# A gated mix of a long-convolution layer and an MLP mixer: plain weight loads, early sines, evictions on ScalarE, and another order of the work

## The chip, the cores and the metric

The kernel runs on one core of a Trainium2 chip. The engines of a core work side by side, each through its own queue in order: TensorE (PE, with its weight load PEld), VectorE (DVE), ScalarE (ACT), GpSimd (POOL) and SyncE (SP), which issues most DMAs. ACT and POOL issue some as well. Waits between engines are semaphores that the framework sets from the data and from the reuse of buffers. The metric is the device time of one launch in microseconds, as the median of several runs.

## The reference

With x of 2048 positions by 640 columns (the batch is 1), all in bf16:

```python
g = sigmoid((x * gate_w).sum(-1))
# a: short causal convolution of k with 4 taps, times v, then a long convolution
kv = sum_t(k shifted by 3 - t, times shift_k) * v
y  = irfft(rfft(kv, 4096) * rfft(ssm_k, 4096))[:2048] + kv * ssm_D
a  = x * y
# b: mixer
h  = gelu(layernorm(x) @ w1)            # 640 -> 640
hs = concat(h[0:160] one later, h[160:320] one earlier,
            h[320:480] two later, h[480:640] two earlier) @ w2
x1 = x + hs
b  = x1 + gelu(layernorm(x1) @ w3) @ w4 # 640 -> 1536 -> 640
out = g * a + (1 - g) * b
```

## The kernel before

Position s = 16 p + n lies on partition p, in slot n. So x is 16 tiles u of 128 partitions by 640 columns, held in four tiles Q. The mixer goes over four chunks c of four slots. `norm_stats` (L275) makes mean and variance on DVE (the tiles st, mv) and the power on POOL (ve, rs). `norm_apply` (L288) makes xn on DVE, transposes it on PE into PSUM, and evicts it to XNT, in two pieces (4 and 1 of the 5 blocks of columns), on DVE or ACT by an argument. `first_product` (L331) multiplies by W1 in the column order "blocks 0 to 3 are the first 128 columns of the four shift groups, block 4 the last 32 of each". Its gelu writes blocks 0 to 3 with the shift straight into GS. Block 4 goes through a tile u4, whose four quarters POOL copies to GS. `second_product` (L413) multiplies GS by W2 and DVE adds the sum to Q. `third_product` (L425) makes gelu(. @ W3) into tiles G, and `fourth_product` (L440) multiplies by W4 and DVE adds to Q (L456), or makes the output at the end (L452). Groups of the last three are US[0] to US[3]: slots 2 to 5, 6 to 9, 10 to 13, and 14, 15, 0, 1.

The long convolution is a Fourier transform in two steps of matmuls. `filter_transpose` (L260) turns the five loaded tiles HN of the filter into HTA and HTB, and DROW (ssm_D) is added to its first tap. `short_conv` (L397) makes kv for one group of four slots on DVE, from KT, the taps CJ (POOL copies of a raw load CJR, which takes an XNT buffer) and KHALO (k of the slots before). `step1` (L237) multiplies by F1 for filter and signal: PE L246, eviction to AR on ACT (L90), and an ACT-queue DMA that writes DRAM, SH for the filter and SX for the signal. Sines for the second step are made by `gen_step2` (L190): DVE makes integers in three tiles GEN, and ACT makes M2, G1 and G2 by four sines each (L187). `spectrum` (L519) then loops over t = 0 to 31. `spec_h` (L469, matmul L478) makes the filter's spectrum HS from BH, which an SP DMA reads from SH, and swaps the halves of its partitions by another DMA (L483). `spec_x` (L485, matmul L491) makes the signal's from BX, evicts it to XPB on ACT and multiplies by HS on DVE (L496). `spec_z` (L499, matmul L507) goes back, and its tile psz is evicted to ZG by ACT and DVE in turn, and goes to DRAM (SZ). `y_group` (L552) reads SZ as ZT, makes the last matmuls (L564), and combines with g and Q. The gate takes x again as XQ, in the buffer of GS: `gate_dot` (L357) is one DVE instruction for each of 16 slots (row scr), `gate_act` makes g and 1 - g (OMG), and ACT scales Q by OMG.

Order: code is emitted in the order in which the program text asks for it, and a scheduler of the framework reorders a little between engines. `merge(a, b, ratio)` (L589) takes a step of generator a, then as many steps of b as a's cost times the ratio pays for. Pools give buffers in turn under a tag: the tag "w" has three large ones (W1 and W2 together, HTA, W3, W4, XPB), "b5" eleven of four slots, "g" three (HN, GEN, later G), "xnt" two. PSUM has two buffers under "pm" (the mixer) and two under "pc" (everything of the convolution). A tile waits until the last use of the one whose buffer it takes.

Before, `signal()` (L613) runs convolution g and, between its pieces, step 1 of g - 1. The filter's step 1 is merged with the second product of US[0], then come first products 2 and 3 with the first convolution and the sines, then a merge of `mixer_front` with the signal at 0.6, then the spectrum merged with a third and a fourth product at 0.75, and the rest of these is emitted after it. A third product follows the last psz, and then the y groups and the last fourth product.

Of the kernel before, what the change touches and what calls it, by code (L numbers as in the profile page):

```python
# [17 lines left out]
def kernel(  # L18
# [25 lines left out]
    nc = tc.nc  # L44
# [73 lines left out]
    load_q(0)  # L118
    load_h(0)
    load_q(1)  # L120
    load_h(1)
    W12 = weights("W12", [P, 2, DT, D])
    W1P = W12[:, 0]
    W2P = W12[:, 1]
    w1v = B_w1.rearrange("(kt p) n -> p kt n", p=P)
    pieces = [(gi * P, P, gi * CG) for gi in range(4)] + [(4 * P + gi * R, R, gi * CG + P) for gi in range(4)]
    with nc.allow_non_contiguous_dma(reason="weight permutation"):
        for (nn, cnt, oo) in pieces:
            nc.sync.dma_start(out=W1P[:, :, nn:nn + cnt], in_=w1v[:, :, oo:oo + cnt])
    load_h(2)  # L130
    load_q(2)
# [26 lines left out]
    def gen_tile():  # L158
        t = main.tile([P, 1024], I32, name="GEN", tag="g", bufs=3)
        return t[:]  # L160
# [29 lines left out]
    def gen_step2():  # L190
        GA, GB, GC = gen_tile(), gen_tile(), gen_tile()
# [13 lines left out]
        for name, kl in (("f", klf), ("i", kli)):  # L205
            ms = consts.tile([P, 2, 4], F32, name="ms" + name)
            for a, amp in ((0, 2 * PI_ / TU), (1, -PI_)):
                for j in range(4):
# [6 lines left out]
        nc.gpsimd.iota(ick.rearrange("p (g i n) -> p g i n", i=4, n=16), pattern=[[64, 8], [4, 4], [0, 16]],  # L215
                       base=0, channel_multiplier=0)
        nc.gpsimd.iota(icn.rearrange("p (m n) -> p m n", n=16), pattern=[[0, KH], [1, 16]],
                       base=0, channel_multiplier=0)
# [4 lines left out]
        yield 0.0  # L223
        nc.vector.scalar_tensor_tensor(out=m1, in0=ick, scalar=basei[:], in1=icn, op0=ALU.add, op1=ALU.mult)
# [31 lines left out]
    DROW = row("DROW")  # L256
    nc.gpsimd.dma_start(out=DROW[0:1, :], in_=A_ssm_D.rearrange("(a d) -> a d", a=1))
# [50 lines left out]
    for gi, sh in enumerate(shifts):  # L308
        for b in (range(0, sh) if sh > 0 else range(N2 + sh, N2)):
            col = 0 if sh > 0 else P - 1  # L310
            nc.gpsimd.memset(GS[:, gi, b, col:col + 1], 0.0)
            nc.gpsimd.memset(GS[gi * R:(gi + 1) * R, 4, b, col:col + 1], 0.0)
# [18 lines left out]
    def first_product(c, XNT):  # L331
        for nts in ((4,), (0, 1), (2, 3)):
            ps = ps_tile("psw1", "pm")
            for j, nt in enumerate(nts):
                for dt in range(DT):
                    nc.tensor.matmul(ps[:, j, :], lhsT=W1P[:, dt, nt * P:(nt + 1) * P], rhs=XNT[:, dt, :],  # L336
                                     start=(dt == 0), stop=(dt == DT - 1))
# [19 lines left out]
    def gate_dot(u):  # L357
        scr = row("scr")
        nc.vector.scalar_tensor_tensor(out=scr[:], in0=XQ[:, u, :], scalar=1.0, in1=GWB[:],  # L359
                                       op0=ALU.mult, op1=ALU.mult, accum_out=Z32[:, u:u + 1])  # L360
# [79 lines left out]
    def fourth_product(us, G, last):  # L440
        for i, u in enumerate(us):
# [13 lines left out]
            else:  # L455
                nc.vector.tensor_tensor(out=halves(qu), in0=ps[:, :, 0:HD], in1=halves(qu), op=ALU.add)  # L456
            yield 1.6
# [27 lines left out]
    def spec_x(t):  # L485
# [7 lines left out]
        xp = XPB[:, t % 4]  # L493
# [21 lines left out]

    AH = 5
    LAST = []

    def spectrum():  # L519
# [6 lines left out]
        for t in range(n):  # L526
# [4 lines left out]
            if t in (1, 2, 5, 6):  # L531
                g = (1, 2, 5, 6).index(t)
                nc.sync.dma_start(out=XQ[:, 4 * g:4 * g + 4, :], in_=qv[:, 4 * g:4 * g + 4, :])
            if 4 <= t < 4 + N2:
                gate_dot(t - 4)
            if t == 4 + N2:
                gate_act()
            if t > 4 + N2:
                done_ = [u for us in US[0:3] for u in us]
                for u in (done_[t - 5 - N2:t - 4 - N2] if t < n - 1 else done_[t - 5 - N2:]):  # L540
                    qu = Q[u // 4][:, u % 4, :]
                    evac("a", qu, qu, OMG[:, u:u + 1])
# [9 lines left out]
    def y_group(g, early):  # L552
# [6 lines left out]
        for i in range(4):  # L559
# [8 lines left out]
            nc.vector.tensor_tensor(out=ty[:], in0=ty[:], in1=XQ[:, u, :], op=ALU.mult)  # L568
            qu = Q[u // 4][:, u % 4, :]
            if u in early:  # L570
                evac("a", qu, qu, OMG[:, u:u + 1])
                nc.vector.tensor_tensor(out=qu, in0=qu, in1=ty[:], op=ALU.add)
            else:
                fin = edge("fin")
                nc.vector.tensor_tensor(out=fin[:], in0=qu, in1=ty[:], op=ALU.add)
                nc.sync.dma_start(out=outv[:, u, :], in_=fin[:])
# [12 lines left out]
    def merge(a, b, ratio):  # L589
# [11 lines left out]
        for _ in b:  # L601
            pass

# [9 lines left out]
    def signal():  # L613

        prev = iter(())
        for g in range(NG):
            if 1 < g + 1 < NG:
                load_kv(g + 1)
            if g == 1:
                nc.sync.dma_start(out=W4[:], in_=B_w4.rearrange("(kt p) e -> p kt e", p=P))  # L620
            for c_ in short_conv(g):
                yield c_
                next(prev, None)
                next(prev, None)
            run(prev)
            prev = step1(xrows(g), SX, g)
        for c_ in prev:
            yield c_

# [3 lines left out]

    c4 = [[4 * c + i for i in range(4)] for c in range(NG)]
    st0 = norm_stats(tiles_of(c4[0]))
    filter_transpose(0)
    X0 = norm_apply(tiles_of(c4[0]), st0, "v")
    st1 = norm_stats(tiles_of(c4[1]))
    CJ = load_cj()
    filter_transpose(1)  # L640
    with nc.allow_non_contiguous_dma(reason="weight permutation"):
        for (nn, cnt, oo) in pieces:
            nc.sync.dma_start(out=W2P[nn % P:nn % P + cnt, nn // P, :], in_=B_w2[oo:oo + cnt, :])
    load_h(3)
    load_q(3)
    KHALO = load_halo()
    load_h(4)
    load_kv(0)
    X1 = norm_apply(tiles_of(c4[1]), st1, "v")
    run(first_product(0, X0))  # L650
    filter_transpose(2)
    st2 = norm_stats(tiles_of(c4[2]))
    filter_transpose(3)
    run(first_product(1, X1))
    filter_transpose(4)
    W3 = weights("W3", [P, DT, Fh])
    nc.sync.dma_start(out=W3[:], in_=B_w3.rearrange("(kt p) f -> p kt f", p=P))
    load_kv(1)
    sig = signal()
    X2 = norm_apply(tiles_of(c4[2]), st2, "v")  # L660
    gen = gen_step2()
    next(gen)
    merge(second_product(US[0]), filt(), 1.0)
    next(sig)
    sy0 = norm_stats(tiles_of(US[0]))
    next(sig)
    run(first_product(2, X2))
    next(gen)
    st3 = norm_stats(tiles_of(c4[3]))
    next(sig)  # L670
    next(gen)
    Y0 = norm_apply(tiles_of(US[0]), sy0, "v")
    X3 = norm_apply(tiles_of(c4[3]), st3, "v")
    W4 = weights("W4", [P, FT, D])
    run(first_product(3, X3))

    def mixer_front():
# [4 lines left out]
        Y1 = norm_apply(tiles_of(US[1]), sy1, "v")  # L682
        yield 3.0
        yield from fourth_product(US[0], G_[0], False)
        yield from second_product(US[2])
        sy2 = norm_stats(tiles_of(US[2]))
        yield 4.4
        yield from third_product(Y1, G_[1])
        Ys.append(norm_apply(tiles_of(US[2]), sy2, "v"))
        yield 3.0  # L690
        yield from second_product(US[3])
        sy3 = norm_stats(tiles_of(US[3]))
        yield 4.4
        yield from fourth_product(US[1], G_[1], False)
        Ys.append(norm_apply(tiles_of(US[3]), sy3, "v"))

    Ys = []
    merge(mixer_front(), sig, 0.6)
    XPB = weights("XPB", [P, 4, 3, D])
    XQ = main.tile([P, N2, D], BF16, name="XQ", tag="gs")  # L700
    third3 = third_product(Ys[1], G_[3])
    merge(spectrum(), chain(third_product(Ys[0], G_[2]), fourth_product(US[2], G_[2], False)), 0.75)
    with tc.issue_after(LAST[-1].ins):
        run(third3)
# [33 lines left out]
```

## Time and profile before

| quantity | us |
|---|---|
| median of 3 runs | 320.95 |
| lowest, highest | 318.3, 322.01 |
| the profiled execution | 321.86 |
| its span | 320.1 |

The profile is of the execution of 321.86 us; 1.76 us of it lie outside the span. All times below are counted from the start of the span. The costliest groups of instructions on ACT, DVE and PE are:

| group (line, engine, tile) | count | busy us | mean ns |
|---|---|---|---|
| L445 PE, fourth product, 128x320 | 384 | 59.1 | 299 |
| L432 PE, third product, 128x512 | 240 | 56.9 | 391 |
| L90 ACT, AR from step 1, 128x640 | 64 | 40.3 | 694 |
| L496 DVE, XPB products, 128x640 | 64 | 28.5 | 487 |
| L326 ACT, gelu to G, 128x1024 | 24 | 24.8 | 1031 |
| L336 PE, first product, 128x512 | 100 | 27.9 | 434 |

A matmul's mean counts from its own issue and overlaps its neighbours, so that work is priced below by the spacing of instructions that follow each other without a wait. In a row of the timeline or of a group, "out<-in" names the tiles, "x8" counts the instructions, and the bracket at the end has the idle time before and what ended it.

Of transfers, the page gives the time from issue to landing: W (1920 KB) 12.7 us, SH<-AR 3.3, BX<-SX 5.1, BH<-SH 4.8, HS<-HS 2.6.

### The profile page before, as it was taken

To read this page: it belongs to the slowest core of one execution; us is meant where nothing else is said; L and a number is where in the kernel's file an instruction comes from. 1 tells how busy PE (TensorE), PEld (TensorE's weight loads), DVE (VectorE), ACT (ScalarE), POOL (GpSimd) and SP (SyncE) were. 2 spreads that over 40 slices of the span, in tenths; PEclk is the share of its full clock that TensorE was granted. 3 is DMA by queue.
4 is the path that set the end of the run, shared out by engine and by line. 5 is a ranking of instruction groups with operands and counts; after the bars stand their busy time and mean duration, and the time that the engine had idled before them with its cause. 6 is when DMAs were issued, how large, how long until landed. Compare 5 with 4: busy or idle time off the path is not lost.

```text
span 320.1 us, 4302 instructions
## 1 busy us (share of the span) xinstructions
PE 256.1 (80%) x1572; PEld 151.4 (47%) x1572; DVE 207.4 (65%) x433; ACT 174.3 (54%) x250; POOL 33.5 (10%) x68
## 2 busy tenths in 40 slices
PE   1538989762079999999989969999966664899995
PEld 1424565331045546764556634566633332445673
DVE  4889669711993983799988980465565554500982
ACT  1221559999715262226635048979876674445750
POOL 3362611500003110002001000000000000000000
PEclk9965999997559999999999989999997999599999
DMA  7999900679600242022227935487789865259741
GB/s 244 255 318 376 402 7 0 245 244 368 210 2 0 82 163 84 2 82 82 84 82 239 402 83 182 123 258 236 217 283 264 288 204 180 82 171 405 248 174 72
DMA packets 32787, 59.59 MB, mean 186 GB/s; under 512 B 7391, under 2 KB 23903, under 8 KB 32766
## 3 DMA queue, kind: packets, MB, share of 16 engines
q1 hardware_dynamic: 19870, 42.77, 40.9%
q10 hardware_dynamic: 12672, 15.73, 13.3%
q0 software_dynamic: 224, 0.82, 0.8%
q8 instruction: 12, 0.20, 0.3%
q14 instruction: 9, 0.07, 0.1%
HBM read 35.71 MB, written 18.35 MB: 169 GB/s over the span
## 4 chain that ended last, share of the span: by engine, by line
PE 51%; DVE 22%; DMA 9%; ACT 7%; issue 2%; DVEq 0%; SPq 0%; ACTq 0%
PE psw L432 13%; PE psw L445 10%; PE psw L336 8%; PE psz L507 6%; DVE acc L407 4%; PE psw L418 4%; DMA BX<-SX 4%; DMA SH<-AR 3%; DVE tmp L405 3%; PE psy L564 3%; ACT AR L90 3%; DMA XQ<-in_A_q_dram 3%; PE psx L491 2%; PE psh L478 2%; DVE scr L359 2%; ACT HS L92 2%
## 5 line engine op out<-in xcount | busy, mean ns | idle before, releaser
L445 PE MATMUL psw<-W,G 128*128 128x320 bf16 x384 | 59.1, 299 | 0.1
L432 PE MATMUL psw<-XNT,W 128*128 128x512 bf16 x240 | 56.9, 391 | 0.0
L90 ACT CAST AR<-ps 128x640 bf16<-128x640 f32 x64 | 40.3, 694 | 26.4 <-PE ps L246 26.1
L496 DVE TENSOR_TENSOR XPB<-XPB,HS 128x640 bf16<-128x640 bf16 x64 | 28.5, 487 | 33.5 <-ACT XPB L90 33.5
L445 PEld LDWEIGHTS <-G 128*128 128x128 bf16 x384 | 37.5, 98 | 15.7 <-issue 1.0
L326 ACT ACTIVATE G<-psw 128x1024 bf16<-128x1024 f32 x24 | 24.8, 1031 | 24.7 <-PE psw L432 24.7
L432 PEld LDWEIGHTS <-W 128*128 128x128 bf16 x240 | 24.1, 101 | 27.9 <-issue 3.2
L92 ACT ACTIVATE HS<-psh 128x640 bf16<-128x640 f32 x32 | 22.8, 719 | 23.3 <-PE psh L478 23.3
L301 PE MATMUL pst<-IDB,xn 128*128 128x128 bf16 x160 | 14.3, 253 | 22.1 <-DVE XNT L95 13.0
L280 DVE BATCH_NORM_STATS2 st<-Q 128x6 f32<-128x320 bf16 x64 | 27.5, 466 | 4.2 <-DMA Q<-in_A_q_dram 4.2
L336 PE MATMUL psw<-XNT,W 128*128 128x512 bf16 x100 | 27.9, 434 | 2.3 <-DVE XNT L95 2.3
L507 PE MATMUL psz<-XPB,G 128*128 128x320 bf16 x128 | 25.6, 328 | 4.9 <-ACT HS L92 3.1
L90 ACT CAST XPB<-psx 128x640 bf16<-128x640 f32 x32 | 22.4, 700 | 7.0 <-PE psx L491 6.8
L418 PE MATMUL psw<-W,GS 128*128 128x320 bf16 x160 | 22.7, 299 | 1.6 <-DVE XNT L95 1.0
L301 PEld LDWEIGHTS <-xn 128*128 128x128 bf16 x160 | 12.3, 114 | 24.5 <-issue 17.7
L491 PE MATMUL psx<-BX,M 128*128 128x320 bf16 x64 | 15.3, 324 | 7.8 <-DMA BX<-SX 3.1
L507 PEld LDWEIGHTS <-G 128*128 128x128 bf16 x128 | 13.4, 105 | 15.9 <-issue 9.6
L246 PEld LDWEIGHTS <-F 128*128 128x128 bf16 x128 | 12.2, 97 | 17.6 <-issue 10.7
L294 DVE TENSOR_SCALAR xn<-Q,mv,rs 128x640 bf16<-128x640 bf16 x32 | 15.8, 536 | 5.9 <-POOL rs L285 5.9
L418 PEld LDWEIGHTS <-GS 128*128 128x128 bf16 x160 | 15.6, 98 | 8.4 <-issue 2.2
L95 DVE CAST ZG<-psz 128x640 bf16<-128x640 f32 x16 | 13.1, 821 | 9.3 <-PE psz L507 9.3
L336 PEld LDWEIGHTS <-W 128*128 128x128 bf16 x100 | 10.9, 110 | 16.5 <-issue 9.0
(104 smaller groups left out, 335.6 us busy)
## 6 DMA issues: line engine op xcount, KB each, us to landing
SH<-AR ACTq DMA_DIRECT2D x8, 640.0 KB, 3.3
SX<-AR ACTq DMA_DIRECT2D x8, 640.0 KB, 3.1
BH<-SH SPq DMA_DIRECT2D x8, 640.0 KB, 4.8
HS<-HS SPq DMA_DIRECT2D x32, 160.0 KB, 2.6
BX<-SX SPq DMA_DIRECT2D x8, 640.0 KB, 5.1
SZ<-ZG ACTq DMA_DIRECT2D x8, 640.0 KB, 3.5
ZT<-SZ SPq DMA_DIRECT2D x8, 640.0 KB, 5.9
W<-in_B_w_dram SPq DMA_DIRECT2D x2, 1920.0 KB, 12.7
```

Source lines behind the costliest of these rows:

```text
L90: nc.scalar.copy(out=o, in_=i)
L92: nc.scalar.activation(out=o, in_=i, func=ACT.Copy, scale=scale)
L280: nc.vector.bn_stats(out=st[:, h, :], in_=src[i][:, h * HD:(h + 1) * HD])
L301: nc.tensor.transpose(out=pst[:, dd, i * P:(i + 1) * P], in_=xns[i][:, (d0 + dd) * P:(d0 + dd + 1) * P], identity=IDB[:])
L326: nc.scalar.activation(out=o, in_=i, func=ACT.Gelu_apprx_tanh)
L336: nc.tensor.matmul(ps[:, j, :], lhsT=W1P[:, dt, nt * P:(nt + 1) * P], rhs=XNT[:, dt, :], start=(dt == 0), stop=(dt == DT - 1))
L418: nc.tensor.matmul(ps[:, h, 0:HD], lhsT=GS[:, nt, u, :], rhs=W2P[:, nt, h * HD:(h + 1) * HD], start=(nt == 0), stop=(nt == DT - 1))
L432: nc.tensor.matmul(ps[:, j, :], lhsT=W3[:, dt, (f + j) * P:(f + j + 1) * P], rhs=XNT[:, dt, :], start=(dt == 0), stop=(dt == DT - 1))
L445: nc.tensor.matmul(ps[:, h, 0:HD], lhsT=G[ft // 4][:, ft % 4, i * P:(i + 1) * P], rhs=W4[:, ft, h * HD:(h + 1) * HD], start=(ft == 0), sto ...
L491: nc.tensor.matmul(ps[:, h, 0:HD], lhsT=M2[:, t].rearrange("p a b c -> p (a b c)"), rhs=BX[kg][:, i, h * HD:(h + 1) * HD], start=True, sto ...
L496: nc.vector.tensor_tensor(out=xp[:, 1 + a, :], in0=xp[:, 0, :], in1=HS[t // 2][:, a, t % 2, :], op=ALU.mult)
L507: mm = nc.tensor.matmul(pz[:, h, 0:HD], lhsT=gm[:, t].rearrange("p a b c -> p (a b c)"), rhs=XP[t][:, 1 + a, h * HD:(h + 1) * HD], start=( ...
```

## The change

- W1 comes in its own column order by one DMA, right behind the first part of x, instead of eight DMAs that permute it. The matmul reads the first 128 columns of each group as the slice `nt * CG` to `nt * CG + P`, and the last 32 of each group are gathered by one ACT copy into W1E. W2 comes by two DMAs instead of eight.
- `gen_step2` has its integers in a "w" buffer (GENW) instead of three "g" buffers, and is started before anything else: M2's sines come ahead of X0's eviction, G1's after it, G2's after X1.
- Every eviction of XNT goes to ACT instead of DVE.
- The memsets of GS's edges on POOL, DROW's load and the loads of CJ and KHALO come later, and the order of loads and first products is another.
- The four first products with the first second product come before the filter's step 1, which is now run together with the first two short convolutions in `conv_front`; x's step 1 follows it.
- W4's load goes from the SP queue to the ACT queue, behind the filter's last write.
- `mixer` holds all second products, third products 0 to 2 and fourth products 0 to 2, in another order. What is left of it when `conv_front` ends goes beside the spectrum (ratio 1.5). XQ is loaded by four POOL DMAs after the last second product.
- The gate dots are asked for from t = 14 instead of t = 4, and Q is scaled by OMG as soon as its tile is summed (`summed`, `scaled`).

```diff
+    W1N = W12[:, 0]
+    nc.sync.dma_start(out=W1N, in_=B_w1.rearrange("(kt p) n -> p kt n", p=P))
...
-        for (nn, cnt, oo) in pieces:
-            nc.sync.dma_start(out=W1P[:, :, nn:nn + cnt], in_=w1v[:, :, oo:oo + cnt])
...
+    nc.scalar.copy(out=W1E.rearrange("p k (g r) -> p k g r", r=R),
+                   in_=W1N.rearrange("p k (g c) -> p k g c", c=CG)[:, :, :, P:CG])
+    def w1_cols(dt, nt):
+        return W1E[:, dt, :] if nt == 4 else W1N[:, dt, nt * CG:nt * CG + P]
+    def load_w2():
+        nc.sync.dma_start(out=W2P[:, 0:4, :], in_=bass.AP(
+            tensor=B_w2.tensor, offset=B_w2[0, 0].offset, ap=[[D, P], [CG * D, 4], [1, D]]))
+        nc.sync.dma_start(out=W2P[:, 4, :], in_=bass.AP(
+            tensor=B_w2.tensor, offset=B_w2[P, 0].offset, ap=[[CG * D, 4], [D, R], [1, D]]))
...
+    GENW = main.tile([P, 3, 1024], I32, name="GEN", tag="w", bufs=3)
...
-        GA, GB, GC = gen_tile(), gen_tile(), gen_tile()
+        GA, GB, GC = GENW[:, 0, :], GENW[:, 1, :], GENW[:, 2, :]
...
+    def conv_front():
+        rows = filt()
+        for g in range(NG):
+            if 1 < g + 1 < NG:
+                load_kv(g + 1)
+            if g == 2:
+                nc.scalar.dma_start(out=W4[:], in_=B_w4.rearrange("(kt p) e -> p kt e", p=P))
+                rows = chain(step1(xrows(0), SX, 0), step1(xrows(1), SX, 1))
+            if g == 3:
+                rows = step1(xrows(2), SX, 2)
             for c_ in short_conv(g):
                 yield c_
-                next(prev, None)
-                next(prev, None)
-            run(prev)
+                for _ in range(4 if g < 3 else 2):
+                    next(rows, None)
+            if g > 0:
+                run(rows)
+        for c_ in step1(xrows(3), SX, 3):
             yield c_
...
+    gen = gen_step2()
+    next(gen)
     st0 = norm_stats(tiles_of(c4[0]))
...
-    X0 = norm_apply(tiles_of(c4[0]), st0, "v")
+    X0 = norm_apply(tiles_of(c4[0]), st0, "a")
+    gs_edges()
+    next(gen)
+    load_w2()
...
+    run(first_product(0, X0))
+    X1 = norm_apply(tiles_of(c4[1]), st1, "a")
+    next(gen)
+    CJ = load_cj()
...
+    run(second_product(US[0]))
+    run(first_product(2, X2))
...
+    def mixer():
         yield from second_product(US[1])
...
         yield from fourth_product(US[0], G_[0], False)
+        yield from third_product(Y1, G_[1])
         yield from second_product(US[2])
...
         yield from second_product(US[3])
+        Y2 = norm_apply(tiles_of(US[2]), sy2, "a")
...
+        XQ.append(main.tile([P, N2, D], BF16, name="XQ", tag="gs"))
+        for g in range(NG):
+            nc.gpsimd.dma_start(out=XQ[0][:, 4 * g:4 * g + 4, :], in_=qv[:, 4 * g:4 * g + 4, :])
         yield from fourth_product(US[1], G_[1], False)
+        yield from third_product(Y2, G_[2])
+        Ys[0] = norm_apply(tiles_of(US[3]), sy3, "a")
+        yield from fourth_product(US[2], G_[2], False)
+    merge(conv_front(), mix, 1.0)
+    XPB.append(weights("XPB", [P, 4, 3, D]))
+    merge(spectrum(), mix, 1.5)
+    run(mix)
     with tc.issue_after(LAST[-1].ins):
-        run(third3)
+        run(third_product(Ys[0], G_[3]))
```

## The prediction

> **What bounds it now.** I read the page's busy shares first, then the chain that ended last, and cut the span at the chain's own milestones: the end of the first second product (51.03 us), the first third product (106.2; its first matmul in the chain is at 106.35), the wait for XQ (169.95), the loop's first psz (201.84), the end of the psz that still have filler beside them (231.9) and the start of the last third product (279.84).
>
> ```profile
> PE 256.1 (80%) x1572; PEld 151.4 (47%) x1572; DVE 207.4 (65%) x433; ACT 174.3 (54%) x250; POOL 33.5 (10%) x68
> ...
> PEclk9965999997559999999999989999997999599999
> ...
> PE 51%; DVE 22%; DMA 9%; ACT 7%; issue 2%; DVEq 0%; SPq 0%; ACTq 0%
> ```
> PE is busiest, but only half of the chain is PE. Where the other half lies is seen stage by stage (columns: stretch, its length, busy time of each engine, granted clock, DMA share, GB/s):
>
> ```profile
> 0.00:51.03 51.03, 33.40 (x235) 22.27 (x236) 38.70 (x125) 17.34 (x26) 19.64 (x48) 0.87 0.74 251
> 51.03:92.71 41.68, 21.09 (x126) 11.43 (x126) 26.02 (x49) 34.45 (x48) 5.21 (x8) 0.80 0.59 205
> 92.71:106.20 13.49, 13.49 (x70) 7.24 (x70) 8.56 (x14) 5.36 (x10) 2.89 (x6) 0.84 0.13 32
> 106.20:169.95 63.75, 61.22 (x396) 36.61 (x394) 53.88 (x81) 27.88 (x37) 4.50 (x4) 1.00 0.22 77
> 169.95:201.84 31.89, 29.33 (x183) 17.11 (x181) 20.21 (x51) 15.30 (x24) 1.26 (x2) 0.95 0.64 226
> 201.84:231.90 30.06, 30.06 (x200) 19.31 (x200) 16.77 (x32) 26.21 (x41) 0.00 (x0) 1.00 0.74 222
> 231.90:279.84 47.94, 31.33 (x155) 15.90 (x153) 25.88 (x51) 29.19 (x46) 0.00 (x0) 0.87 0.68 217
> 279.84:320.10 40.26, 36.22 (x221) 21.58 (x219) 17.35 (x37) 18.57 (x23) 0.00 (x0) 0.97 0.58 213
> ```
> Three stretches leave PE unused: the first two (38 us idle) and the 48 us after the filler ran out (17 idle). Inside and just behind the second, the timeline's rows of PE (two) and ACT (two) show the hole (start, length, engine, line; in brackets the idle time before and its releaser):
>
> ```profile
> 89.13 2.29 PE L301 MATMUL pst<-IDB,xn 128*128 128x128 bf16 x20 [12.96 <-DVE XNT L95]
> 92.71 3.57 PE L336 MATMUL psw<-XNT,W 128*128 128x512 bf16 x8 [1.29 <-DVE XNT L95]
> ...
> 75.75 1.28 ACT L187 ACT_TABLE_LOAD   x1
> 77.04 9.16 ACT L187 ACTIVATE G<-GEN,msi 128x1024 bf16<-128x1024 int32 x8
> ```
> PE waits 13 us for an XNT eviction that stands behind a short convolution on DVE, with the sines on ACT meanwhile. The chain has, before that, "ACT AR" pieces and 9.96 us of SH's write (the convolution's buffers), and later "BX<-SX" 5.80 and 6.35 in the loop without filler.
>
> **Prices** (spacing of back-to-back instructions): matmul 0.136 us (320 wide), 0.216 (512), 0.427 at half clock; so a first product is 5.4 per four tiles, second 5.6, third 13.0, fourth 13.1, step 1 8.7 for the filter and 8.7 for x, one t of the spectrum 1.09. ACT: AR 0.63, gelu 0.95, sine 1.15, table load 1.28, an XNT eviction estimated from 128x512 (585 ns) and 128x1024 (1031) at 1.9 + 0.6. DVE: convolution 10 per group, Q add 0.73.
>
> **To the end of the first second product: 51.0 becomes 57.4.** ACT first gathers W1's fifth block (one copy of 128x640, 0.7 as AR) while it has nothing else. M2's four sines run at about 15 to 19.5, in a gap of ACT, then X0's eviction (2.5), so the first product starts at about 21.4, 5.5 earlier than its 26.92. Behind it on ACT stand G1's sines to 26.5, HTB evictions, gelus and G2's sines cut up by gelus: of 12 sines (13.8 us) eight lie between X0's eviction and the second product, and five table loads (6.4) lie in this stretch. The second first product ends at about 47. The chain is then elsewhere: CJ's raw load goes out on POOL only at about 39.3, behind a statistic of the third norm, and lands 5.5 later (its row); four CJ copies (0.75 each) make 47.8; KHALO's memset 1.9; four u4 copies into GS 2.6: 52.3. The second product waits for those copies: 52.3 + 5.6 = 57.9, of which I give back half a microsecond for what the copies overlap: 57.4. Queued behind PE's wait is everything of PE, so this is lost in full. Bounds: 52 (sines under DMA waits) to 61 (the CJ load at the 9.0 of XQ).
>
> *A rule against this edit.* The trace has a load at 52.76 to 54.04, straight after an AR eviction that ends at 52.74, and the gelu starts at 54.05: 1.3 in all. The Trainium skill, "ScalarE: Activation LUTs", section "What ACT_TABLE_LOAD costs", has the 1.28 too, but adds about 1.38 of drain to every switch. By that page an estimate for the five switches is some 7 us more. The row shows no such drain, and the sum goes by the row.
>
> **To the first third product: 106.2 becomes 80.** Without the convolution and the sines ahead of it: first product 5.4, X3's transposes and eviction 3.4, first product 5.4, Y0 2.8, second product 5.6 = 22.6 from 57.4. The convolution of group 0 now lies on DVE beside it (66.6 to 76.6), and four Q adds behind Y0's xn. This stretch was 55.2 us before and is the gain: 32.6. The eviction on ACT is 0.9 dearer than the 1.6 of DVE's rows (1218 + 415 ns), 7 us over eight XNT, but no longer queues behind convolution pieces; that is where the 13 us went.
>
> **Filter step 1 beside the third product: 80 to 108.5.** Here the old cover is gone: step 1 had the hole to itself. ACT does 27 AR (17.0), six gelus (5.7), an XNT (2.5): 25.2; with a wait of about 3 for SH's write (3.3 in its row) or for the convolution's buffers 28.5. PE has 13.0 + 8.7, so ACT is the bound.
>
> **W4: to 118.5.** Its load moves from SP, issued at 68.2 and long hidden, to ACT's queue behind the last SH write, since it takes HTA's buffer, which the filter's step 1 reads until then. Queued behind it are x's AR evictions; their own matmuls are later, so the issue (0.37) holds nobody. Issued at 108.5 to 109, it lands 7 (its 1.97 MB at the 260 to 280 GB/s of busy slices) to 12.7 us later (W's row, issued among other loads); I take 9.5, as kv loads run beside it. The fourth product waits, PE idle about 6 (4 to 11) with a few AR matmuls in it; it starts on the half clock, as at 92.71 (15 matmuls in 5.47 instead of 3.2).
>
> **Fourth, third, x's step 1: to 153.3**: 13.1 + 13.0 + 8.7 = 34.8. Convolutions 2 and 3 end at about 126 and 146.5 and come in time.
>
> **Two second products, XQ, to the first psz: 178.** The adds and statistics are DVE's, eight adds at 0.73, sixteen st at 0.43, eight mv at 0.1: 13.5 us, to 166.8. Only then is XQ's buffer (GS) free, as at 169.95 before; four POOL transfers land after 5.5 (CJR) to 9.0 (XQ from SP), as no row shows POOL loading as much; I take 7.5, between them, as the load is split alike. The code puts the gate dots at t = 14, but the order of DVE's queue has five of them ahead of the loop's first XPB product. So the change's gate move does not do what it says: 166.8 + 7.5 + five dots of 0.74 = 178.0. Up to here 23.8 us are gained (201.84 before).
>
> **The loop: 78.0 becomes 79.** PE's work beside it grows to the rest of one fourth (10.5), a third (13.0) and a fourth product (13.1): 36.6 us, 1.18 per t, so 2.27 per t with the spectrum's own. Before, the first 11 t carried 17.4 of filler (1.58 per t) with PE full at 2.67 per t; the other 20 took 2.4 with the two BX waits. ACT has 2.13 per t, DVE 1.9. I take 2.55: 31 x 2.55 = 79. Bounds 2.27 and 2.75, 70 to 85. So a net 19 us of PE work more than before stands in the loop and costs 1, because it fills the 17 idle; that is where the time of the front comes from.
>
> **The tail: 40.3**, the same instructions: third, y groups, fourth.
>
> Sum: 178.0 + 79 + 40.3 = 297.3 against a span of 320.1. With the 1.76 us of the profiled execution outside its span 299.1; that execution (321.86) is 0.91 above the median, so 298.1: **298**.
>
> The plain W1 and W2 loads (3 transfers for 16) save SP 11.83 us of issue for the first eight, but PE begins on X0's eviction, not on W1; cost and gain nothing, cover the sines before it. If W1 came later than 21.4, it would cost what it is late by; 0.82 MB at 251 GB/s is 3.3. DROW and the GS memsets move behind norm statistics on POOL, in a stretch where POOL is 20 of 51 busy: nothing.
>
> **Rivals.**
> *The loop turns into the bound (slower).* One t holds psh, psx and psz in the same two PSUM buffers, with ACT and DVE between them and now a gelu or Q scale in ACT's queue all the way. From 178 + 31r + 40.3 = 320.1 the sign turns at r = 3.28 us per t; at 3.4 the span is 323.7 and the time 324.6. Against it: 2.67 with more filler per t. For it: BX waits of 6 us recurred, and a wait of 6 at every second of the eight groups is 0.8 per t. 0.12.
> *The front gives back half.* The W4 load takes 12.7 (+3.2) and PE returns at half clock (+1.5, the row below), XQ 9 (+1.5), CJ the upper bound (+3.6), ACT's wait in step 1 doubles (+3): 12.8, so 311. 0.2.
> *W4 and XQ at their lower bounds, loop at PE's 2.27:* -2.5, -2, -8.6: 285. 0.13.
> *Front and loop losses cancel the gain*, 318 to 324: 0.06.
> *The forecast:* 0.49, of its own range 290 to 306.
>
> *Clock.* PE idle from 76 to 89 shows 0.50 granted in 80 to 96, and the matmuls there cost 1.5 us more in the row above. The Trainium skill, "TensorE: Matmul & The Clock Gate", section "HAM oscillation — how this bites in real kernels", warns of idle gaps over about 3.4 us. By it, an estimate is that W4's and XQ's waits, both longer, each cost such a return: with the row's 1.5, some 3 us more than the sum has.
>
> About 1% is what a measurement can tell from no change. Faster by more: 0.49 + 0.13 + 0.2 = 0.82; within 1%: 0.06; slower 0.12. Range: 284 to 316, from the bounds at both ends (the case of the big gain to the upper end of the half-given-back one); it leaves out the last two.
>
> **What would show it.** PE's wait before the first second product released by POOL's GS copies (right) or by a gelu (sines were too dear). No 13 us gap behind DVE XNT. AR evictions back to back at about 80 to 108 with PE's idle time before psw L445 released by W's DMA, 4 to 11 us. Dots right behind XQ's landing at about 174. The spacing of psz over the loop, 2.3 to 2.75 right, above 3.2 the slow rival. A tail other than 40 would make the last term wrong, and a first psz after 190 the first terms.

## The result, and the profile after

The changed kernel takes 303.0 us (median of 4 runs, 302.73 to 304.04) against 320.84 in the same comparison: a ratio of 0.946, 95% interval 0.940 to 0.952. 298 was predicted, with 284 to 316 as the range. The profiled execution took 303.06 with a span of 301.3. Medians here leave out four runs in a slower state, at a lower granted clock (one of run 9, two of run 11, one of run 12).

The prediction went from milestone to milestone, and so can the result be read (us from the start of the span). The order of the work is another, so the same milestone does not have the same work behind it in the two kernels:

| milestone | before | predicted | after |
|---|---|---|---|
| first second product ends | 51.0 | 57.4 | 58.1 |
| first third product starts | 106.2 | 80 | 81.8 |
| first fourth product starts | 123.1 | 118.5 | 120.4 |
| rest of the second products starts | – | 153.3 | 155.8 |
| first psz | 201.8 | 178.0 | 181.5 |
| last third product starts | 279.8 | 257.0 | 261.9 |
| end | 320.1 | 297.3 | 301.3 |

From the page of the kernel after: the busy shares, the granted clock and the chain by engine.

```profile
PE 246.1 (82%) x1559; PEld 148.8 (49%) x1572; DVE 196.1 (65%) x417; ACT 193.9 (64%) x268; POOL 39.1 (13%) x72
...
PEclk9999877999999985799999997999999999999999
...
PE 56%; ACT 15%; DVE 13%; DMA 11%; issue 2%; SPq 1%; POOL 0%; ACTq 0%; DVEq 0%
```

DVE's 22% of the chain before has become 13, ACT's 7 has become 15, and DMA's 9 is now 11: part of the wait moved from DVE to ACT and to a transfer. The windows of the kernel after, cut at its own milestones (stretch, length, busy time of each engine, clock, DMA share, GB/s):

```profile
0.00:58.10 58.10, 33.08 (x229) 21.04 (x232) 40.82 (x142) 39.40 (x45) 22.01 (x50) 0.91 0.63 221
58.10:81.90 23.80, 21.11 (x143) 12.37 (x144) 19.98 (x31) 13.30 (x22) 11.08 (x12) 1.00 0.08 29
81.90:120.44 38.54, 24.62 (x136) 12.48 (x137) 22.23 (x31) 26.51 (x38) 1.26 (x2) 0.88 0.70 239
120.44:155.76 35.32, 35.14 (x203) 20.75 (x205) 21.01 (x19) 19.74 (x29) 0.00 (x0) 0.94 0.39 136
155.76:181.53 25.77, 20.40 (x155) 14.05 (x153) 19.81 (x48) 12.16 (x17) 4.78 (x8) 1.00 0.71 249
181.53:261.91 80.38, 76.54 (x481) 46.84 (x486) 54.77 (x115) 61.49 (x93) 0.00 (x0) 0.98 0.68 213
261.91:301.30 39.39, 35.26 (x218) 21.29 (x218) 17.48 (x37) 21.31 (x27) 0.00 (x0) 1.00 0.58 217
```

The second row looks like the gain: what took 55.2 us with PE idle for 20.6 now takes 23.8 with PE idle for 2.7. But the filter's step 1 and the sines left that stretch as well. The first of them now stands in the third row, which takes 38.5 us up to the first fourth product where the kernel before took 16.9. At that milestone the kernels are only 2.7 us apart (123.1 and 120.4). Added up over all rows ahead of the first psz, PE is idle for 43.3 us before and for 47.2 after. The first psz comes 20.3 us earlier because less is done ahead of it: PE is busy there for 134.4 us instead of 158.5, as the products that stand beside the loop grew from 17.4 us of work to 36.6 (by the prediction's prices). The loop pays for them with its idle time, 16.6 us of PE before and 3.8 after, and is only 2.4 us longer. Over the whole span PE's idle time falls by 8.8 us and its busy time by 10.0, at a mean granted clock of 0.955 instead of 0.918. The convolution's own path had to be early enough for this. The last write of x's step 1 goes out at 163.7 instead of 174.98 (the kernel before, by its timeline, and below it the kernel after, by its tile SX):

```profile
174.98 0.37 ACTq L251 DMA_DIRECT2D SX<-AR  x1
```

```profile
L258 ACTq DMA_DIRECT2D SX<-AR x8: 366/367/367, 124.8 to 163.7; - x8
```

The two longest waits of PE that are left outside the front stand in its timeline and in the chain of waits:

```profile
120.44 3.36 PE L452 MATMUL psw<-W,G 128*128 128x320 bf16 x12 [7.34 <-DMA W<-in_B_w_dram]
181.53 0.83 PE L515 MATMUL psz<-XPB,G 128*128 128x320 bf16 x4 [2.79 <-DVE XPB L504]
```

```profile
109.18 0.49 ACT XNT L90
110.11 10.29 DMA W<-in_B_w_dram
120.44 3.36 PE psw L452 x12
...
171.29 5.86 DMA XQ<-in_A_q_dram
177.25 2.93 DVE scr L366 x7
181.53 0.83 PE psz L515 x4
```

W4 goes out at 110.1 and lands 10.3 later; PE is idle for 7.3, and its first 12 matmuls take 3.36 where 0.136 each would make 1.6. XQ lands at 177.15 (171.29 + 5.86), and dots stand ahead of the first XPB product.

### The profile page after: what moved, and what is told of

It is laid out like the page before. It is cut to its first block, busy times and chain, and to the rows that moved or that the text cites. A ratio compares the mean times of both kernels' runs of the same rounds, so it can differ in the third digit from the quotient of the medians.

```text
span 301.3 us, 4269 instructions
## 1 busy us (share of the span) xinstructions
PE 246.1 (82%) x1559; PEld 148.8 (49%) x1572; DVE 196.1 (65%) x417; ACT 193.9 (64%) x268; POOL 39.1 (13%) x72
## 4 chain that ended last, share of the span: by engine, by line
PE 56%; ACT 15%; DVE 13%; DMA 11%; issue 2%; SPq 1%; POOL 0%; ACTq 0%; DVEq 0%
PE psw L439 17%; PE psw L452 14%; PE psz L515 5%; PE psw L425 4%; PE ps L253 4%; DMA HN<-in_A_ssm_k_dram 3%; DMA W<-in_B_w_dram 3%; PE psw L343 3%; PE psy L576 3%; ACT G L194 3%; PE psx L499 2%; ACT XNT L90 2%; DVE scr L366 2%; DMA XQ<-in_A_q_dram 2%; PE psh L486 2%
## 5 line engine op out<-in xcount | busy, mean ns | idle before, releaser
L452 PE MATMUL psw<-W,G 128*128 128x320 bf16 x384 | 64.9, 308 | 8.6 <-DMA W<-in_B_w_dram 7.3
L439 PE MATMUL psw<-XNT,W 128*128 128x512 bf16 x231 | 57.8, 379 | 1.4 <-ACT G L333 1.0
L504 DVE TENSOR_TENSOR XPB<-XPB,HS 128x640 bf16<-128x640 bf16 x64 | 28.3, 486 | 15.8 <-ACT XPB L90 15.6
L439 PEld LDWEIGHTS <-W 128*128 128x128 bf16 x240 | 23.4, 98 | 23.9 <-issue 1.7
L515 PE MATMUL psz<-XPB,G 128*128 128x320 bf16 x128 | 23.5, 304 | 3.9 <-DVE XPB L504 3.2
L425 PE MATMUL psw<-W,GS 128*128 128x320 bf16 x160 | 24.0, 299 | 2.9 <-ACT XNT L90 1.8
L343 PE MATMUL psw<-XNT,W 128*128 128x512 bf16 x80 | 22.4, 440 | 2.5 <-ACT u L333 2.5
L273 PE MATMUL psh<-IDB,HN 128*128 128x128 bf16 x80 | 8.3, 265 | 16.9 <-DMA HN<-in_A_ssm_k_dram 14.8
L253 PEld LDWEIGHTS <-F 128*128 128x128 bf16 x128 | 12.4, 98 | 15.4 <-issue 8.4
L90 ACT COPY XNT<-pst 128x2048 bf16<-128x2048 bf16 (+1 forms) x16 | 19.0, 1242 | 0.3 <-PE pst L306 0.2
L299 DVE TENSOR_SCALAR xn<-Q,mv,rs 128x640 bf16<-128x640 bf16 x32 | 12.6, 443 | 10.0 <-POOL rs L290 8.4
L515 PEld LDWEIGHTS <-G 128*128 128x128 bf16 x128 | 12.4, 98 | 12.6 <-DVE XPB L504 3.7
L414 DVE TENSOR_TENSOR acc<-acc,tmp 128x2560 bf16<-128x2560 bf16 x12 | 18.3, 1521 | 0.4
L353 POOL COPY GS<-u 32x512 bf16<-32x512 bf16 (+4 forms) x20 | 15.9, 807 | 19.3 <-ACT u L333 18.8
## 6 DMA issues: line engine op xcount, KB each, us to landing
HN<-in_A_ssm_k_dram SPq DMA_DIRECT2D x5, 512.0 KB, 10.3
```

The costliest lines, as they stand in the source:

```text
L90: nc.scalar.copy(out=o, in_=i)
L253: nc.tensor.matmul(ps[:, comp, 0:HD], lhsT=F1[:, comp, :], rhs=src[:, c0:c0 + HD], start=True, stop=True)
L343: nc.tensor.matmul(ps[:, j, :], lhsT=w1_cols(dt, nt), rhs=XNT[:, dt, :], start=(dt == 0), stop=(dt == DT - 1))
L414: nc.vector.tensor_tensor(out=acc[:], in0=acc[:], in1=tmp[:], op=ALU.add)
L425: nc.tensor.matmul(ps[:, h, 0:HD], lhsT=GS[:, nt, u, :], rhs=W2P[:, nt, h * HD:(h + 1) * HD], start=(nt == 0), stop=(nt == DT - 1))
L439: nc.tensor.matmul(ps[:, j, :], lhsT=W3[:, dt, (f + j) * P:(f + j + 1) * P], rhs=XNT[:, dt, :], start=(dt == 0), stop=(dt == DT - 1))
```

## The experiments

Unless a line says otherwise each run is the changed kernel with one edit, timed in three rounds, and the ratio is to the kernel before (0.946 for the change). My theory was: the order of DVE's work around the convolution is the gain; the front pays for it through ACT and POOL; W4 and XQ are waits that the change brings; the loop takes the moved products almost for nothing.

**The front: runs 1, 2 and 5.**

```diff
     gs_edges()
     next(gen)
+    next(gen)          # G2 right behind G1
...
     X1 = norm_apply(tiles_of(c4[1]), st1, "a")
-    next(gen)
```

> The changed kernel, with G2's four sines emitted right behind G1's, ahead of the first gelu: two returns to the sine table fall away, and with them four table loads in the front. If a load costs what its row shows (1.28 us), ACT's chain in the front is 5.1 us shorter; if each switch cost the drain that a page adds (2.66), 10.6. My theory has a second chain close behind: POOL's copies of CJ and of u4 into GS end 1.8 us before the second product starts, so this kernel gains only 1 to 2 us (301 to 302), and the second product is then released by POOL. Rival: POOL's chain is no bound, and the whole 5 us are gained (298).

Run 2 also moves `CJ = load_cj()` and `KHALO = load_halo()` behind `run(first_product(1, X1))`.

> As the run before, and CJ's load, its copies and KHALO's memset are emitted behind the first product of the second chunk, so that POOL copies u4 first. Theory: now the 5 us of the four table loads show (297 to 299 against 303), the first second product ends about 5 us earlier. With a drain behind each switch it would be 292 to 294. Rival: the front is bound elsewhere (DVE's xn and statistics, loads of HN), and no more than 2 us come.

Run 5 has the edit of run 1, CJR in a "b5" buffer instead of "xnt", and `CJ = load_cj()` right behind `st1 = norm_stats(...)`.

> G2's sines behind G1's as in the first run (four table loads less, 5.1 us of ACT), and CJ's raw load in a buffer of its own, emitted behind the second chunk's statistics, so that neither XNT's buffer nor POOL's queue waits for it late. Theory: in the first run X2's transposes ended at 46.85, 3.7 us earlier than in the changed kernel, and then its eviction waited 3.5 us for POOL's CJ copies; without that wait the second product starts at about 49 to 50 instead of 52.5, and the whole takes 299.5 to 301 against 303. Rival: the four table loads were not on the chain at all, and the time stays at 303 or above, with the second product again at 52 or later.

| run | us | ratio, 95% interval | first second product starts |
|---|---|---|---|
| after | 303.0 | 0.946, 0.940 to 0.952 | 52.48 |
| 1 grouped | 306.43 | 0.955, 0.949 to 0.961 | 52.26 |
| 2 grouped, CJ later | 304.68 | 0.951, 0.946 to 0.955 | 49.87, its third tile 55.20 |
| 5 grouped, CJ early | 300.09 | 0.936, 0.928 to 0.943 | 47.95 |

Run 1 missed its forecast of 301 to 302: it is 3.4 us slower than the change, and its second product starts no earlier. The second chain was there, but it did not release PE as the theory had it. ACT's and POOL's timelines of run 1:

```profile
50.34 2.35 ACT L90 COPY XNT<-pst 128x2048 bf16<-128x2048 bf16 x2 [3.54 <-POOL CJ L383]
...
38.50 0.63 POOL L380 DMA_DIRECT2D CJR<-in_A_shift_k_dram  x1
42.06 0.77 POOL L353 COPY GS<-u 32x512 bf16<-32x512 bf16 x1 [2.94 <-ACT u L333]
47.25 3.06 POOL L383 COPY CJ<-CJR 128x640 bf16<-128x640 bf16 x4 [4.41 <-DMA CJR<-in_A_shift_k_dram]
```

X2's eviction waits for CJ's copies, since CJR sits in the XNT buffer that it takes, and CJR lands 8.7 us after its issue, against 4.0 in the kernel after. The scheduler had put W3's load, which waits for the sines' buffer, ahead of KHALO, KT and VT on SP's queue: they all go out from 31.9 to 35, not from 20 on, and share the DMA engines with CJR. Run 2 did only half of what was meant: POOL now copies u4 ahead of CJ, but the scheduler issued CJ's load at 38.8 all the same, and KHALO's memset then held the convolution on DVE, with the second product's own Q adds behind it, so that PE waited 2.5 us for them in its midst. Run 5 takes CJ off the chain and gives 2.9 us.

The table loads: run 5 has two sine-to-gelu returns less than the kernel after, four loads. Its second product starts 4.5 us earlier than in the kernel after, but one part of that is spread. The same front, with edits only behind it, started it at 50.27 in run 3, 50.47 in run 4, 49.77 in run 6 and 53.00 in run 7. PE between 36 and 42 and between 42 and 48 was granted 0.77 and 0.78 in the kernel after, 0.50 and 0.94 in run 3, and 1.00 in both in run 5. With the grouped front of run 5 and of run 9 below it starts at 47.95 and 48.42. So grouping the sines and moving CJ are worth 1.4 to 5.0 us together; no run parts the two. Four loads at 1.28 are 5.1. With the drain of 1.38 that the Trainium skill, "ScalarE: Activation LUTs", section "What ACT_TABLE_LOAD costs", adds to each, an estimate is 10.6. The traces have no room for that: the load at 28.53 of the kernel after takes 1.28, and the gelu behind it starts at 29.83.

**W4: run 3.**

```diff
     def filt():
         for g in range(NG):
             yield from step1(hrows(g), SH, g)
+            if g == 2:
+                nc.scalar.dma_start(out=W4[:], in_=...)   # was in conv_front, behind all of filt()
```

> The changed kernel, with W4's load emitted as soon as the filter's third group is through step 1, the last reader of HTA, and not behind the fourth group. It goes out about 10 us earlier, lands at about 109 to 111, and the fourth product starts right behind the third. Theory: PE's 7.3 us wait goes, and the matmuls at half clock behind it (1 to 1.5 us): 294 to 296 against 303. Rival: the load only moves the bound to ACT's evictions or to x's convolutions, which must come in time for the later second products: less than 3 us.

294.51 us, ratio 0.919 (0.914 to 0.923): 8.5 us less than the change. The load goes out at 97.7, 12.4 earlier, and lands 10.6 later. PE's timeline of run 3:

```profile
110.06 4.69 PE L452 MATMUL psw<-W,G 128*128 128x320 bf16 x21 [1.38 <-ACT XNT L90]
```

The fourth product starts at 110.06 (120.44), the first psz at 171.64 (181.53), and the span is 291.5 (301.3): 10.4 gained at the wait arrive as 9.8 at the end. Nothing behind it took the time back. Of the 10.4 and of the load's 12.4, 1.8 are the front's spread: the first third product already starts at 80.01 (81.81). The theory was right on the wait, and not on the clock: the row's 21 matmuls and two others take 4.69 us where 0.136 each would make 3.1, at 0.64 granted, so the slow start of the fourth product stays. The last reader of HTA is group 2 of the filter, as group 3 lies in HTB; the load was behind both.

**The gate dots and XQ: run 4, and run 10 below.**

```diff
         scr = row("scr")
-        nc.vector.scalar_tensor_tensor(...)
+        with tc.issue_after(LASTX[-1].ins):   # the XPB product of the same step
+            nc.vector.scalar_tensor_tensor(...)
```

> The changed kernel, with each gate dot held on DVE behind the XPB product of its own step, so that XQ's landing no longer stands before the first psz. Theory: the first psz comes 3 to 4 us earlier (177.5 to 178.5 against 181.5) and the whole gains 3 to 4 us: 299 to 300. Rival: PE fills the wait with the fourth product anyway, the loop takes what the start gives, and the time stays within 1.5 us of 303.

312.43 us, 0.977 (0.971 to 0.983): 9.4 us worse than the change, while the first psz does come 5.1 us earlier, at 176.40. Both theories missed it. The chain of waits of run 4, in the loop, and below it two psz that follow each other in PE's timeline of run 4:

```profile
177.63 8.44 DMA BX<-SX
...
241.71 6.29 DMA BX<-SX
...
256.33 4.42 ACT Q L92 x6
...
261.33 1.45 ACT Q L92 x2
```

```profile
252.12 0.43 PE L517 MATMUL psz<-XPB,G 128*128 128x320 bf16 x2
...
259.06 0.71 PE L517 MATMUL psz<-XPB,G 128*128 128x320 bf16 x4
```

The next group's BX is asked for when the loop begins, beside the last of XQ's transfers, and takes 8.4. But that wait is made good: the psz at 252.12 is the 29th, and in the kernel after the 29th starts at 256.17. The time is lost behind it. The dots, held back, make the gate late, at 255.1 instead of 208.8, so that Q's scaling crowds on ACT ahead of the last psz. From the 29th to the 30th psz it takes 6.9 us instead of 2.2. The loop to the end of the last psz takes 88.4 instead of 80.4, and 36 matmuls of a fourth product, 5 us, are left over behind it: the last third product starts at 269.50 (261.91).

**The loop: run 6**, profiled but not timed in rounds.

```diff
-    merge(spectrum(), mix, 1.5)
     run(mix)
+    run(spectrum())
```

> The changed kernel with all of the mixer run ahead of the spectrum, none beside it. Theory: the loop's own pace, without filler, is 2.0 to 2.4 us per t (ACT and the BX reads), so the loop falls from 80.4 to 65 to 74 while the 36.6 us of products stand ahead of it: 303 + 36.6 - 6 to 15 = 325 to 333. Rival: the loop is bound by PE, and the products cost beside it what they cost alone: 303 to 308.

341.29 us in its one execution: above my theory's 325 to 333, and far from the rival's. From the first psz (218.30) to the last third product (300.09) the loop takes 81.8 with nothing beside it; in the kernel after it is 80.4 with 36.6 us of products. The window of run 6, and below it the same window of the kernel before:

```profile
218.30:300.09 81.79, 56.30 (x241) 27.94 (x242) 39.63 (x79) 47.14 (x72) 0.00 (x0) 0.75 0.66 209
```

```profile
201.84:279.84 78.00, 61.39 (x353) 35.22 (x353) 42.65 (x83) 55.39 (x85) 0.00 (x0) 0.92 0.70 219
```

No engine is full: 241 matmuls, 33 us at 0.136 each, keep PE "busy" for 56 us at a granted clock of 0.75, and the chain of these 80 us holds three BX waits (6.45, 6.20, 6.36) and the round psx, XPB, product, psz, ZG through two PSUM buffers. Alone the loop goes at 2.64 us per t, with the products at 2.59. So the products beside it cost nothing here. What sets the pace was not taken apart, and whether the loop would go faster alone at the full clock was not tried. It is no fixed floor: in the kernel before the 11 t with filler took 2.7 each, and the other 20, without, 2.4.

Run 6 also shows what the change lives on. With all 36.6 us ahead of the loop the kernel is 38 us slower than the change, and slower than the kernel before. Beside the loop before stood 17.4. An estimate from this run, with the other 19.2 put back ahead of the loop, is 303 + 19.2 = 322, which would be no gain at all. A kernel in the order of before with more of its products beside the loop was not run.

**The order and the engine of the evictions: runs 7 and 8, and 12 on the kernel before.**

```diff
+    conv = conv_front()
+    for _ in range(5):
+        next(conv)                  # the first convolution, as it stood before
     run(first_product(2, X2))
...
-                for _ in range(4 if g < 3 else 2):
+                for _ in range(0 if g == 0 else 7 if g == 1 else 4 if g < 3 else 2):
                     next(rows, None)
...
-    merge(conv_front(), mix, 1.0)
+    merge(conv, mix, 1.31)
```

> The changed kernel with the first short convolution emitted ahead of the first product of chunk 2, as it stood before (the filter's step 1 still behind, 7 pieces beside each step of the second convolution). Theory: its 10 to 12 us of DVE then stand ahead of the statistics, xn and Q adds that the first products wait for, and PE idles for most of that: 308 to 314. Rival: with the XNT evictions on ACT the place of the convolution no longer matters: 302 to 304.

310.82 us, 0.968 (0.958 to 0.978): 7.8 us lost. The number is the theory's, the way to it is not. The convolution's pieces do stand between Q adds, statistics and xn: the chain goes through "DVE tmp", "DVE acc", "DVE VT" from 55.8 to 66.1, then the statistics and "POOL rs" to 72.4. But PE hardly waits for it. From the end of the first second product to the first third product it takes 24.8 us with PE idle for 3.4, where the kernel after takes 23.7 with 2.7. Most is lost in the next stretch, where this edit also packs the filter's step 1 more closely beside the second convolution: the fourth product starts 8.1 us late (128.56), the third product only 2.2. PE's timeline of run 7:

```profile
83.98 0.81 PE L439 MATMUL psw<-XNT,W 128*128 128x512 bf16 x3
...
124.72 1.29 PE L253 MATMUL ps<-VT,F 128*128 128x320 bf16 x4 [7.35 <-ACT AR L90]
```

So the run does not show that one convolution in the way of the statistics is worth the 7.8.

Run 8 replaces "a" by "v" in all eight `norm_apply` calls; run 12 replaces "v" by "a" in the kernel before.

> The changed kernel with all XNT evictions on DVE again. Theory: in the front ACT is the chain (16.6 to 52.4) and loses three evictions of 2.35 us, while DVE has room: the first second product ends 2 to 4 us earlier; behind it the evictions of X3, Y0 and Y1 stand in DVE's queue beside convolutions, at most one piece of 1.5 us each. Together 299 to 304. Rival: the evictions behind convolutions bring the hole of before back: 308 or more.

> The kernel before with the XNT evictions on ACT alone. In the other kernel their return to DVE cost 6 us. Theory: here ACT is full of AR evictions and then of sines just where the XNT of chunk 3 and Y0 are due, so the hole of 13 us stays mostly: ratio 0.98 to 1.01. Rival: the eviction's place behind the convolution on DVE was the hole itself, and ACT removes it: 0.96 to 0.97.

Run 8: 309.17, 0.965 (0.958 to 0.972), the rival's side: 6 us lost. The front did not get shorter beyond its own spread (second product at 50.54, against 49.77 to 53.00 for the unedited front), and that product then took 7.3 instead of 5.6 at a lower clock. Y1's eviction did stand in DVE's queue behind the second convolution. DVE's timeline of run 8:

```profile
107.66 1.49 DVE L414 TENSOR_TENSOR acc<-acc,tmp 128x2560 bf16<-128x2560 bf16 x1
109.07 1.22 DVE L95 COPY XNT<-pst 128x2048 bf16<-128x2048 bf16 x1
110.20 1.48 DVE L416 TENSOR_TENSOR VT<-acc,VT 128x2560 bf16<-128x2560 bf16 x1
111.60 0.42 DVE L95 COPY XNT<-pst 128x512 bf16<-128x512 bf16 x1
```

W4 went out at 112.15 (110.11), and the fourth product began 12.6 later, at 124.71 (120.44). Half of the 4.3 us is thus W4's slower landing, which was not taken apart. The other half stood already at the first third product, 83.89 (81.81): from there to W4's issue it takes 28.3 us in both kernels, so Y1's wait behind the convolution did not add to it. The rival's number came, its reason is not in the rows.

Run 12: 318.7, 0.993 (0.988 to 0.998). The same edit that is worth 6 us in the new order is worth 2 in the old one. The hole stays: PE is idle for 15.2 us up to 87.89 there, with one XNT eviction now behind the sines on ACT until 85, and the xn of the next behind the convolution on DVE until 84. What ends the idle time is the convolution's last piece, VT, since x's step 1 stands ahead of the transposes on PE. ACT's and PE's timelines of run 12:

```profile
73.56 9.17 ACT L187 ACTIVATE G<-GEN,msi 128x1024 bf16<-128x1024 int32 x8
82.63 2.33 ACT L90 COPY XNT<-pst 128x2048 bf16<-128x2048 bf16 x2
...
87.89 1.25 PE L246 MATMUL ps<-VT,F 128*128 128x320 bf16 x4 [15.21 <-DVE VT L409]
```

**The plain weight loads: run 11**, the kernel before with these alone.

```diff
-        for (nn, cnt, oo) in pieces:
-            nc.sync.dma_start(out=W1P[:, :, nn:nn + cnt], in_=w1v[:, :, oo:oo + cnt])
+    nc.sync.dma_start(out=W1P, in_=B_w1.rearrange("(kt p) n -> p kt n", p=P))
+    nc.scalar.copy(out=W1E..., in_=W1P...)      # and W2 by two DMAs
```

> The kernel before with the plain W1 and W2 loads alone (3 DMAs and a gather on ACT for 16 DMAs). Theory: PE starts on X0's eviction, not on W1, so no gain: ratio 0.993 to 1.007 to before. Rival: the eight W1 pieces held SP for 11.8 us, and HN and Q behind them arrive earlier now: 3 us or more, ratio 0.99 or below.

321.1 us, 1.0013 (0.998 to 1.005): nothing, as predicted.

**Put together: runs 9 and 10.** Run 9 has the edits of runs 3 and 5. Run 10 adds

```diff
-        ... in0=XQ[0][:, u, :], in1=GWB[:] ...
+        ... in0=Q[u // 4][:, u % 4, :], in1=GWB[:] ...
...
     run(first_product(1, X1))
+    for u in c4[0] + c4[1]:
+        gate_dot(u)
...
     run(first_product(2, X2))
+    for u in c4[2] + c4[3]:
+        gate_dot(u)
```

with `gate_act()` at t = 2, Q scaled from t = 3 on, and XQ's loads asked for from t = 14.

> The early W4 load (third run), with G2's sines behind G1's and CJ early (fifth run), in one kernel. Theory: the two gains lie one behind the other on the same chain and add: 303 - 8.5 - 2.9 = 291.6 (290 to 293). Rival: with W4 out of the way the stretch of the filter's step 1 is bound by ACT's evictions and SH's writes, and a front that ends earlier only waits there: 294 to 295.

> As the ninth run, with the gate dots made in the front from Q, which still holds x there, the gate at once behind them, XQ loaded only for the end, and Q scaled as soon as its tile is summed. XQ's landing and five to seven dots no longer stand before the first psz. Theory: DVE has room for the 12 us of dots in the front and the psz start 4 to 6 us earlier; since the loop without filler shows that it goes at its own pace of 2.6 us per t whatever PE has beside it, the end comes earlier by as much: 285 to 288. Rival, after the fourth run: BX of the second group is not there when the loop begins earlier, or the dots push xn back in the front, and the time stays at 291 or above.

| run | us | ratio, 95% interval | second product starts | fourth product | first psz | last third product |
|---|---|---|---|---|---|---|
| 3 | 294.51 | 0.919, 0.914 to 0.923 | 50.27 | 110.06 | 171.64 | 252.1 |
| 9 | 293.92 | 0.917, 0.908 to 0.925 | 48.42 | 109.25 | 170.37 | 250.7 |
| 10 | 292.82 | 0.913, 0.908 to 0.919 | 52.78 | 113.62 | 172.53 | 251.7 |

The gains of runs 3 and 5 do not add: 1.9 us at the second product are 0.8 at the fourth, since the filter's step 1 between them waits for SH's write and the convolution's buffers in both (the chain of run 9 has "DMA SH<-AR" at 90.0 and then "DVE tmp", "DVE acc"). In run 10 the dots cost the front 4.4 us, and behind it the stretch from the fourth product to the first psz is 2.2 shorter and the loop 1.2 (79.2): the sum is within the noise of runs 3 and 9. Run 10 also did not do all that its text says: POOL issued XQ's loads from 164.5 to 170.3 all the same, ahead of the first psz at 172.53. All three beat both kernels; which of them is best these runs do not tell.

## Why the prediction was right, and where it was not

**The gain.** Two reasons were given. The first was the order: the convolution and the sines out of the way of statistics, xn and evictions between the first second product and the first third product. The stretch was put at 22.6 and took 23.7. As a sum of terms that is right. As a cause it is only argued: run 7 puts one convolution back and this stretch grows by 1.1, run 12 shows that the eviction's engine alone does not close the hole, and no run puts the filter's step 1 or the sines back. Nor was the hole of 13 us the queue alone: in DVE's timeline of before the convolution itself waits 7.4 us for SH's write, up to 78.98 and 2.8 us into the hole. The second reason was the net 19 us of PE work that goes into the loop and costs 1 there. That is the one which the rows and run 6 bear out: 20.3 us at the first psz, 2.4 more in the loop, and 38 us lost when the products are taken out of it. Run 8 shows that the eviction's engine matters in the new order. For this the prediction had no term of its own, only the words that the eviction no longer queues behind convolution pieces.

**The first second product, 57.4 against 58.1, right for partly the wrong reason.** The prediction let the second product be released by POOL's copies of u4 at 52.3, behind a late CJ. It was ACT: X2's eviction from 50.56 to 52.44, at the end of sines, table loads and gelus, and POOL's copies ended at 50.72. The two chains lie within 2 us. In run 1, with ACT's shorter, CJ's copies held X2's eviction, and nothing was gained; in run 5 both are out of the way. The step of CJ was right as a second bound, not as the first.

**W4's wait, 6 us and a cold clock, measured 7.3 and 1.7.** The load was put at 108.5 to 109 and 9.5, and came at 110.1 and 10.3. For the return at half clock the prediction wrote 1.5 and left it out of the sum; its own row, 15 matmuls in 5.47 us instead of 3.2, makes it 2.2. It held the buffer to be busy until the end of the filter's step 1. Run 3 shows that this was some 10 us too late, and that the wait was avoidable, though not the slow matmuls behind it.

**XQ and the dots: 3.5 us more than predicted.** 2.5 were carried over from the stages before. XQ's load was released at 171.3 instead of 169.3 (the 166.8 of the sum and the 2.5), as xn came between the adds (+2.0); it took 5.9 instead of 7.5 (-1.6); and the five dots, 3.7, were followed by an XPB product (+0.6). That the dots stand ahead of it in DVE's queue in spite of t = 14 was right.

**The loop, 79 against 80.4.** The size was right, its reason half: I had it between PE's 2.27 and 2.75 per t, as if PE's work still set the pace. Run 6 takes 2.6 without any product beside it. The rival of a loop at 2.27 did not come either: counted from the first psz to the last third product no run went below 2.5 per t. The slow rival, 3.28 per t and more from BX waits, did not come; run 4, with two BX waits and the late scaling, reached 2.85.

**The tail, 40.3 against 39.4**, and the plain loads at nothing (run 11) were as predicted. The sum of the terms is 4.0 us short of the span: 0.7, 1.1, 0.1, 0.6, 1.0 and 1.4 from stage to stage, less 0.9 in the tail. Every stage but the last ran a little longer than its sum of back-to-back spacings.

## What to carry to other kernels

When a change moves work about, add up PE's idle time over all stages and see where the work went before one stage is called the gain: here the stage that shrank by 31 us gave nearly all of it back in the stages beside it, and the gain was what had moved beside the loop. A loop in which no engine is full can take other products: here it took 36.6 us of them in the time that it needed without them, and what is moved there comes off the rest of the kernel. When work is held back for the start of a loop, as the dots were, see what waits for it at the loop's end. A load into a buffer that comes free late should be issued right behind that buffer's last reader, not behind the stage that reader belongs to.

## What was not expected of the hardware

- The same front, unedited or with edits only behind it, started its second product between 49.77 and 53.00 us in five executions. What differs in the rows is the granted clock. With pauses of 1.2 to 2.8 us of PE behind ACT, all five show 0.50 to 0.8 over 3 us or more, but in other windows. It is not the pause alone: in run 5 PE pauses for 4.2 us before 24.56 and is granted 1.00 all through the front. The cause stays open.
- Without filler the loop is granted 0.75 (run 6), with it 0.98. Its pace per t is nearly the same, 2.64 and 2.59.
- One 0.64 MB load, CJR, landed after 4.0 to 4.2 us where little else was under way, and after 8.5 to 8.7 beside W3, KT and VT at some 410 GB/s (runs 1 and 2).
